# Chunk-batches 7 to 23 of a fused linear-attention and MLP kernel: transposes moved from TensorE to the DMA queue, and a planner that paces the input loads

## The chip, the cores and the metric

The kernel runs on one core of a Trainium2 chip. The metric is device time in microseconds (us) of that core for the whole kernel; the time of a kernel is the median of several executions. One further execution was taken with the hardware profiler, and all durations of single instructions come from it.

## What is computed

A gated linear attention (four batches, eight heads, 768 steps, head size 48) feeds a two-layer MLP with a squared ReLU. Cut to what matters:

```python
def _attn_ref(r, k, v, w, u):                       # all [4, 8, 768, 48], u [8, 48]
    state = zeros((B, H, D, D))
    for t in range(S):
        cur = einsum('bhd,bhe->bhde', u * kt, vt)
        y[:, :, t] = einsum('bhd,bhde->bhe', rt, state + cur)
        state = wt[..., None] * state + einsum('bhd,bhe->bhde', kt, vt)
def _moe_ref(x, w_in, w_out, s, b):                 # x [3072, 384], w_in [384, 2048]
    r = maximum(x @ w_in, 0.0)
    return (s * (r * r) + b) @ w_out
```

`x` is `y` with the heads side by side, one row for each token. Inputs and outputs are float32; the kernel computes in bfloat16 with float32 accumulation.

## The kernel before

**Tiling.** The sequence is cut into 6 chunks of 128 steps. A chunk of one batch is a *chunk-batch*; there are 24 of them, numbered n = 0 to 23, with the batch running fastest, so that chunk-batch n needs the state that n - 4 left. Two chunk-batches make one MLP tile T (256 tokens, 12 tiles).

**One chunk-batch.** SyncE (SP) loads w, r, k and v, 192 KB each (`load`, L225). ScalarE (ACT) takes the logarithm of w (`ln`, L232), TensorE (PE) forms running sums of it (`cum`, L281 to L289), ACT exponentiates them (`expo`, L303), and VectorE (DVE) multiplies them into r and k (`mult`, L313): the result `prd` has time on the partitions. The score product needs it with features on the partitions, so it is transposed into `RK`. There are two ways to do that, chosen by the constant `DTK`:

- n < `DTK`: `trans` (L340) is eight TensorE transposes into PSUM, and `tevac` (L355) is an ACT copy of the 128x1024 result into SBUF;
- n >= `DTK`: `dtrans` (L362) is one DMA crossbar transpose, SBUF to SBUF, issued by SP.

Then come the scores (`mt`, L382, PE), the causal mask (`mask`, L394, DVE), the output (`ymm`, L410 and L419, PE) and its evacuation into `x_sb` (`yevac`, L449, DVE). `x_sb` is transposed into `xT`, the input of the MLP, again in two ways chosen by `DTX`: `xtr` and `xevac` (L497, three TensorE transposes, and L512, an ACT copy), or `dxtr` (L372, one DMA transpose from SP). In the kernel before both constants are 16. GpSimd (POOL) forms the diagonal term from r, k, u and v (L237, L248, L268) and scales the state (L486); it also casts v to bfloat16 (`castv`, which calls `cast`, L636), the engine being chosen by `VBE`.

**The MLP.** For each tile, `g1` is 8 groups of 6 matmuls into `h_ps` (L546), each group followed by `relu` (L559, ACT) and `square` (L571 on DVE or L569 on ACT); `g2` is 8 groups of 4 matmuls into `o_ps` (L584), and after each 128 tokens `oevac` (L594, DVE) and `store` (L608, SP). The weights are loaded by SP after the inputs of chunk-batch 3 and cast once.

**Order.** Nothing is scheduled at run time. Every engine executes its instructions in the order in which they were issued by the program, and that order is the work of a list scheduler, `Plan`. Each operation is registered with `add`: engine, occupancy `occ`, dependences `deps`, buffers that it takes (`takes`), a priority, a latency, and `slack`, which is added to the end of what it depends on. `order` repeatedly takes the operation that can start earliest and writes it out. A DMA has a cost `dma` on one shared modelled DMA queue, whose end time is the variable `dma`. SP is one of the engines: its loads, transposes and stores stand in one fixed order, and a transpose or a store at its head whose input isn't there holds up everything behind it.

Of the kernel before, what the change touches and what calls it, by code (L numbers as in the profile page):

```python
# [18 lines left out]
U_AT = 3.5  # L19
CIE = 'APAP'  # L20
COE = 'DDDD'
VBE = 'P'
WARM = 28.0
DTK = 16
DTX = 16
SQE = 'DA'
SQT = 2
MSL = 0.1
SLACK = 0.3


class Plan:
# [7 lines left out]
        self.ops = {}  # L40

    def add(self, name, eng, occ, fn, args=(), deps=(), takes=(), prio=0.0,
            lat=0.12, port=False, dma=0.0, slack=0.0):
        self.ops[name] = dict(
            name=name, eng=eng, occ=occ, fn=fn, args=args, deps=list(deps),
            takes=list(takes), prio=prio, lat=lat, port=port, dma=dma,
            slack=slack, after=None, n=len(self.ops),
        )

    def order(self):  # L50
        ops = self.ops
        end = {}
        free = {}
        port = 0.0
        dma = 0.0
        held = {tag: [] for tag in self.rings}
        queues = {}
        for o in sorted(ops.values(), key=lambda o: (o["prio"], o["n"])):
            queues.setdefault(o["eng"], []).append(o)
        out = []  # L60

        def ready(o):
            t = 0.0
            for d in o["deps"]:
                if d not in end:
                    return None
                if d == o["after"]:
                    continue
                own = ops[d]["eng"] == o["eng"] and not ops[d]["dma"]
                t = max(t, end[d] - ops[d]["lat"] if own else end[d] + o["slack"])  # L70
            for tag, _ in o["takes"]:
                h = held[tag]
                if len(h) >= self.rings[tag]:
                    for d in h[-self.rings[tag]]:
                        if d not in end:
                            return None
                        t = max(t, end[d] + o["slack"])
            return t

        while any(queues.values()):  # L80
            best = None
            for eng, q in queues.items():
                e = free.get(eng, 0.0)
                pick = None
                for o in q:
                    r = ready(o)
                    if r is None:
                        continue
                    ask = max(r, e)
                    t = max(ask, port) if o["port"] else ask  # L90
                    if pick is None or t < pick[0] - 1e-9:
                        pick = (t, ask, o)
                if pick and (best is None or pick[:2] < best[:2]):
                    best = pick
            assert best is not None, [q[0]["name"] for q in queues.values() if q]
            t, _, o = best
            queues[o["eng"]].remove(o)
            free[o["eng"]] = t + o["occ"]
            if o["port"]:
                port = t + o["occ"]  # L100
            fin = t + o["occ"] + o["lat"]
            if o["dma"]:
                dma = max(dma, t + o["occ"] + 1.0) + o["dma"]
                fin = dma + 0.9
            end[o["name"]] = fin
            for tag, last in o["takes"]:
                held[tag].append(last)
            out.append((t, o))
        self.end = end
        self.last = out  # L110
        return out
# [3 lines left out]
def kernel(  # L115
# [137 lines left out]
    def castv(n):  # L253
        c = cb[n]
        vb = work.tile([128, H, D], BF16, name="vb", tag="vb", bufs=6)
        cast(VBE[n % len(VBE)], vb, c["v"])
        c["vb"] = vb
# [374 lines left out]
    def cast(letter, out, in_):  # L632
        if letter == "A":
            nc.scalar.copy(out=out, in_=in_)  # L634
        elif letter == "P":
            nc.gpsimd.tensor_copy(out=out, in_=in_)  # L636
        else:
            nc.vector.tensor_copy(out=out, in_=in_)
# [18 lines left out]
    for n in range(N):  # L657
# [3 lines left out]
        P = 10.0 * n  # L661
        SL = SLACK if n > 5 else 0.0
        add(("ln", n), "ACT", 0.45, ln, (n,), [("load", n, 0)] + ([("ln", n - 1)] if n else []),
            [("lw", [("cum", n)])], P)
        add(("rkp", n), "POOL", 1.0, pool1, (n,), [("load", n, 1), ("load", n, 2)],
            [("rkp", [("rku", n)])], P, port=True)
        add(("rku", n), "POOL", 1.0, pool1b, (n,), [("rkp", n), "load_u"],
            [("rku", [("cd", n)])], P, port=True)
        e = CAST[VBE[n % len(VBE)]][0]
        add(("vb", n), e, 0.48, castv, (n,), [("load", n, 3)],  # L670
            [("vb", [("ymm", n)] + ([("dmm", n)] if keep else []))], P,
            port=e == "POOL")
# [10 lines left out]
            + ([("mul", n - 1)] if n else []),  # L683
            [("prd", [("tr" if n < DTK else "tev", n)] + ([("dmm", n)] if keep else []))], P - 1, port=True)
        if n < DTK:
            add(("tr", n), "PE", 0.44, trans, (n,), [("mul", n)],
                [("B", [("tev", n)]), ("RK", [("mt", n), ("ymm", n)])], P - 3,
                lat=0.2, slack=SL)
            add(("tev", n), "ACT", 0.92, tevac, (n,), [("tr", n)], [], P - 3)
        else:  # L690
# [8 lines left out]
            + ([("sup", n)] if keep else [("supn", n)]),  # L699
            [("B", [("yev", n)]), ("x", [("xtr" if n < DTX else "xev", n)])], P - 6, lat=0.2, slack=SL)  # L700
        add(("yev", n), "DVE", 0.48, yevac, (n,), [("ymm", n), ("yd", n)], [], P - 7)
        xt = [("xT", [("g1", T, NQ - 1)])] if j == 0 else []
        xd = [("xev", n - 1)] if j else []
        if n < DTX:
            add(("xtr", n), "PE", 0.17, xtr, (n,), [("yev", n)],
# [21 lines left out]
    for T in range(NT):  # L727
        P = BIG + 10 * T
        for i in range(NQ):
# [5 lines left out]
                + ([("gT", [("g2", T, 4 * CPT - 1)])] if i == 0 else []),  # L735
                P, lat=0.2, slack=MSL if T > 1 else 0.0)
            add(("relu", T, i), "ACT", 0.52, relu, (T, i), [("g1", T, i)],
# [4 lines left out]
        for i in range(4 * CPT):  # L742
# [8 lines left out]
            if part == 0:  # L751
                need.append("colsum")
                take = [("h" if T == NT - 1 else "o", [("oev", T, tt)])]
            add(("g2", T, i), "PE", 0.65, g2, (T, i), need, take, P + 1000 + i, lat=0.2, slack=MSL if T > 1 else 0.0)
            if part == 3:
# [10 lines left out]
    for n in range(N):  # L766
        for x in range(4):
            take = {0: [("w", [("ln", n)])],
                    1: [("rk", [("rkp", n), ("mul", n)])], 2: [],
                    3: [("v", [("vb", n), ("yd", n)])]}[x]  # L770
            chain.append((10.0 * n + x, ("load", n, x)))
            add(("load", n, x), "SP", 0.6, load, (n, x), [], take,
                10.0 * n + x, dma=1.03)
    for i in range(NPIECE):
        chain.append((WIN_AT[i] + 0.01 * i, ("li", i)))
        chain.append((WOUT_AT[i] + 0.01 * i, ("lo", i)))
# [81 lines left out]
```

The softmax here doesn't subtract the row's maximum and nothing guards it: scores larger than these inputs give would overflow.

## Time and profile before

| | |
|---|---|
| median of three runs | 200.1 us (200.05 to 200.14) |
| the profiled execution's own time | 200.52 us |
| its span, first to last instruction | 198.7 us |
| granted TensorE clock | 1.000 |
| busy: PE, ACT, DVE, POOL | 187.0, 133.2, 133.1, 114.4 us |
| `trans`, L340: 128 TensorE transposes; `tevac`, L355: 16 copies | 9.8 us; 16.1 us |
| `xtr`, L497: 48 TensorE transposes; `xevac`, L512: 16 copies | 5.3 us; 7.5 us |
| `castv` on POOL, L636: 24 casts | 13.4 us |
| DMA transposes from SP: `RK` 8, `xT` 8 | 3.4 us and 2.3 us from issue to landing (median) |

PE is TensorE's matmuls, PEld its weight loads; SPq is SyncE's queue, where DMAs are issued. A group's line gives busy time, and after it the mean duration of one instruction in nanoseconds. The DMA share is the mean busy share of the core's 16 DMA engines. It is the sum of the packets' own times, and since packets overlap it goes above 1.

### The profile page before, as it was taken

The numbers are of one execution on the slowest core, as the hardware profiler recorded it, in microseconds if no ns is written. First come the engines' busy times: TensorE is split into PE (matmuls) and PEld (weight loads), VectorE is DVE, ScalarE is ACT, GpSimd is POOL, SyncE is SP. The second block draws the span as 40 slices with busy tenths as digits, with TensorE's granted clock in tenths as the row PEclk, the third lists the DMA queues.
The fourth block names the chain that finished last, engine by engine and source line by source line (L and its number), as shares of the span: only waits on it lengthen the run. The fifth ranks groups of instructions, "written<-read, shape, count | busy, mean of one in ns | idle before, by whom it ended". The sixth has DMA issues, their size and how long they took to land.

```text
span 198.7 us, 4921 instructions
## 1 busy us (share of the span) xinstructions
PE 187.0 (94%) x1928; PEld 138.9 (70%) x1928; DVE 133.1 (67%) x212; ACT 133.2 (67%) x240; POOL 114.4 (58%) x144
## 2 busy tenths in 40 slices
PE   6997888979999999999999999999999999999992
PEld 4766567745668777777776786776687778777651
DVE  6476838836977978869787686799787692222221
ACT  3446487745658999999996997690069868768000
POOL 3787932029998899959987788959981000000000
PEclk9999999999999999999999999999999999999999
DMA  6999999979999999999999899999433931111122
GB/s 125 200 175 179 299 394 371 278 145 200 188 156 197 160 195 173 200 234 195 220 169 194 186 202 190 210 236 173 128 82 75 122 98 27 43 40 40 43 79 79
DMA packets 119239, 33.29 MB, mean 168 GB/s; under 512 B 112432, under 2 KB 117680, under 8 KB 119216
## 3 DMA queue, kind: packets, MB, share of 16 engines
q1 hardware_dynamic: 119216, 32.98, 83.0%
q8 instruction: 15, 0.25, 0.6%
q14 instruction: 8, 0.07, 0.1%
HBM read 25.36 MB, written 4.72 MB: 151 GB/s over the span
## 4 chain that ended last, share of the span: by engine, by line
PE 66%; DMA 14%; SPq 11%; ACT 3%; POOL 2%; issue 2%; DVE 1%; POOLq 0%
PE o_ps L584 26%; PE h_ps L546 23%; SPq L225 9%; DMA wi_st<-in_moe_w_in_dram 5%; DMA wt<-in_w_dram 5%; DMA rkt<-in_k_dram 4%; PE mt_ps L382 3%; PE o_psh L584 3%; PE trps L340 2%; PE y_ps L419 2%; PE y_ps L410 2%; PE cums L281 1%; PE cums L284 1%; PE d_ps L435 1%; ACT rh L559 1%
## 5 line engine op out<-in xcount | busy, mean ns | idle before, releaser
L546 PE MATMUL h_ps<-xT,w_in 128*128 128x256 bf16 x576 | 73.9, 273 | 2.0 <-ACT w_in L634 1.4
L559 ACT ACTIVATE rh<-h_ps 128x512 bf16<-128x512 f32 x96 | 56.2, 598 | 23.2 <-PE h_ps L546 21.8
L584 PE MATMUL o_ps<-w_out,gT 128*128 128x384 bf16 x352 | 66.3, 326 | 0.0
L546 PEld LDWEIGHTS <-w_in 128*128 128x128 bf16 x576 | 53.7, 98 | 12.5 <-issue 1.8
L584 PEld LDWEIGHTS <-gT 128*128 128x128 bf16 x384 | 35.8, 98 | 19.2
L571 DVE TENSOR_TENSOR gT<-rh 128x512 bf16<-128x512 bf16 x56 | 29.4, 537 | 14.5 <-ACT rh L559 14.4
L237 POOL TENSOR_TENSOR rkp<-rkt 128x384 f32<-128x384 f32 x24 | 25.1, 1047 | 17.2 <-DMA rkt<-in_k_dram 17.1
L394 DVE TENSOR_TENSOR mt_sb<-mt_ps,tri_strict 128x1024 bf16<-128x1024 f32 x24 | 29.2, 1216 | 1.3 <-PE mt_ps L382 1.3
L268 POOL TENSOR_TENSOR yd<-vt,cd 128x384 bf16<-128x384 f32 x24 | 25.2, 1048 | 4.8 <-DVE cd L262 4.6
L313 DVE TENSOR_TENSOR prd<-rkt,E 128x768 bf16<-128x768 f32 x24 | 24.1, 1004 | 5.6 <-ACT E L303 4.1
L569 ACT ACTIVATE gT<-rh 128x512 bf16<-128x512 bf16 x40 | 25.2, 630 | 1.3
L248 POOL TENSOR_TENSOR rku<-rkp,u_bc 128x384 f32<-128x384 f32 x24 | 24.6, 1025 | 0.4
L303 ACT ACTIVATE E<-cums 128x768 bf16<-128x768 f32 x24 | 19.4, 806 | 7.5 <-PE cums L289 7.4
L594 DVE SCALAR_TENSOR_TENSOR o_sb<-o_ps,s_bc,bconst 128x384 f32<-128x384 f32 x22 | 13.5, 615 | 14.8 <-PE o_ps L584 13.4
L486 POOL TENSOR_TENSOR st<-stmp,l 128x384 bf16<-128x384 bf16 x16 | 18.6, 1164 | 8.3 <-DVE stmp L477 7.9
L355 ACT COPY RK<-trps 128x1024 bf16<-128x1024 bf16 x16 | 16.1, 1008 | 5.5 <-PE trps L340 5.5
L449 DVE TENSOR_TENSOR x_sb<-y_ps,yd 128x384 bf16<-128x384 f32 x24 | 13.3, 552 | 6.7 <-PE y_ps L419 5.2
L262 DVE TENSOR_REDUCE cd<-rku 128x8 f32<-128x384 f32 x24 | 13.0, 542 | 6.8 <-POOL rku L248 6.8
L232 ACT ACTIVATE logw<-wt 128x384 bf16<-128x384 f32 x24 | 12.4, 523 | 7.0 <-DMA wt<-in_w_dram 6.8
L816 PE MATMUL warm_ps<-warm_sb 128*128 128x256 bf16 x104 | 15.1, 294 | 1.1 <-DVE warm_sb L795 1.1
L636 POOL CAST vb<-vt 128x384 bf16<-128x384 f32 x24 | 13.4, 558 | 0.0
L816 PEld LDWEIGHTS <-warm_sb 128*128 128x128 bf16 x104 | 10.2, 105 | 2.7 <-DVE warm_sb L795 1.1
(52 smaller groups left out, 168.5 us busy)
## 6 DMA issues: line engine op xcount, KB each, us to landing
wt<-in_w_dram SPq DMA_DIRECT2D x24, 192.0 KB, 4.5
rkt<-in_r_dram SPq DMA_DIRECT2D x24, 192.0 KB, 4.4
rkt<-in_k_dram SPq DMA_DIRECT2D x24, 192.0 KB, 4.6
vt<-in_v_dram SPq DMA_DIRECT2D x24, 192.0 KB, 4.4
out_dram<-o_sb SPq DMA_DIRECT2D x24, 192.0 KB, 2.2
wi_st<-in_moe_w_in_dram SPq DMA_DIRECT2D x4, 768.0 KB, 8.3
wo_st<-in_moe_w_out_dram SPq DMA_DIRECT2D x4, 768.0 KB, 7.6
u_bc<-in_u_dram SPq DMA_DIRECT2D x1, 192.0 KB, 4.3
```

Of the source, the lines that this page charges most:

```text
L237: nc.gpsimd.tensor_tensor(out=rkp, in0=c["rk"][:, 0].rearrange("t h d -> t (h d)"), in1=c["rk"][:, 1].rearrange("t h d -> t (h d)"), op=AL ...
L248: nc.gpsimd.tensor_tensor(out=rku.rearrange("t h d -> t (h d)"), in0=c["rkp"], in1=u_bc, op=ALU.mult)
L268: nc.gpsimd.tensor_tensor(out=yd, in0=c["v"], in1=c["cd"].unsqueeze(2).to_broadcast([128, H, D]), op=ALU.mult,)
L303: nc.scalar.activation(out=E, in_=ps[:, :, 0:HD], func=AF.Exp)
L313: nc.vector.tensor_tensor(out=prd[:, :, :, 0:D].rearrange("t x h d -> t (x h) d"), in0=c["rk"].rearrange("t x h d -> t (x h) d"), in1=c["E ...
L394: nc.vector.tensor_tensor(out=m.rearrange("s g p t -> s (g p) t"), in0=c["mt_ps"].rearrange("s g p t -> s (g p) t"), in1=tri_strict.unsque ...
L546: nc.tensor.matmul(ps[:, f, :], lhsT=w_in_sb[ft // FPP][:, kt, (ft % FPP) * 128 : (ft % FPP + 1) * 128], rhs=xT[T][:, kt, :], start=(f == ...
L559: nc.scalar.activation(out=rh, in_=hs[T, i], func=AF.Relu)
L569: nc.scalar.activation(out=g, in_=rh, func=AF.Square)
L571: nc.vector.tensor_tensor(out=g, in0=rh, in1=rh, op=ALU.mult)
L584: nc.tensor.matmul(ps, lhsT=gT[T][:, ft, tt * 128 : (tt + 1) * 128], rhs=w_out_sb[ft // FPP][:, ft % FPP, :], start=(ft == 0), stop=(ft == ...
L816: nc.tensor.matmul(warm_ps, lhsT=warm_sb[:, 0:128], rhs=warm_sb, start=True, stop=True)
```

## The change

Five things change. `DTK` goes from 16 to 7 and `DTX` from 16 to 8, so that nine more chunk-batches (7 to 15) have r and k transposed by DMA, and eight more (8 to 15) have x transposed by DMA. `VBE` goes from 'P' to 'AP': the cast of v is done by ACT for even n and by POOL for odd n. `MSL`, the slack that the planner adds before a group of MLP matmuls (tiles 2 and later), goes from 0.1 to 0.2. And the planner gets a new field, `pace`: a load of chunk-batch 4 or later isn't planned before the modelled DMA queue is within 2.0 us of being drained. `pace` adds no instruction and no wait to the program; it acts only through the order in which the operations are written out.

```diff
-VBE = 'P'
+VBE = 'AP'
 WARM = 28.0
-DTK = 16
-DTX = 16
+DTK = 7
+DTX = 8
 SQE = 'DA'
 SQT = 2
-MSL = 0.1
+MSL = 0.2
+PACE = 2.0
 SLACK = 0.3
...
     def add(self, name, eng, occ, fn, args=(), deps=(), takes=(), prio=0.0,
-            lat=0.12, port=False, dma=0.0, slack=0.0):
+            lat=0.12, port=False, dma=0.0, slack=0.0, pace=0.0):
...
-            slack=slack, after=None, n=len(self.ops),
+            slack=slack, pace=pace, after=None, n=len(self.ops),
...
                     ask = max(r, e)
+                    if o["dma"] and o["pace"]:
+                        ask = max(ask, dma - o["pace"])
                     t = max(ask, port) if o["port"] else ask
...
             add(("load", n, x), "SP", 0.6, load, (n, x), [], take,
-                10.0 * n + x, dma=1.03)
+                10.0 * n + x, dma=1.03, pace=PACE if n > 3 else 0.0)
```

## The prediction

> **What bounds the kernel now.** I read the busy shares and slices of the page first, then the groups of instructions, the table of stretches, and last the SyncE queue in order of time.
>
> ```profile
> PE 187.0 (94%) x1928; PEld 138.9 (70%) x1928; DVE 133.1 (67%) x212; ACT 133.2 (67%) x240; POOL 114.4 (58%) x144
> ...
> PE   6997888979999999999999999999999999999992
> ...
> DMA  6999999979999999999999899999433931111122
> ```
>
> PE is full from slice 10 (about 46 us) to 195 us, while the DMA engines are full until about 140 us and nearly empty afterwards. The first 46 us belong to loads and weights; the change hardly touches them.
>
> ```profile
> 60.00:70.00 10.00, 10.00 (x128) 8.16 (x126) 8.18 (x13) 9.69 (x19) 8.51 (x12) 1.00 1.15 179
> ...
> 80.00:90.00 10.00, 10.00 (x122) 7.72 (x119) 7.75 (x12) 9.72 (x20) 7.87 (x11) 1.00 1.08 215
> 90.00:100.00 10.00, 9.68 (x113) 7.50 (x112) 8.32 (x13) 9.42 (x20) 9.47 (x12) 1.00 1.13 206
> 100.00:110.00 10.00, 9.35 (x112) 7.23 (x111) 8.07 (x13) 8.21 (x17) 8.26 (x11) 1.00 1.16 191
> ```
>
> The columns are the stretch, its length, then PE, PEld, DVE, ACT, POOL, clock, DMA share and GB/s. From 60 to 120 us four resources are close to full at once: PE at 93 to 100%, ACT at 82 to 99%, POOL at 79 to 95%, DMA above 1. PE loses about 1 us in 90 to 110. "Busy" could flatter PE, since matmuls overlap; but in the chain of waits the steps follow one another at their full-rate length (6 matmuls of 256 columns 0.66 us, 4 of 384 columns 0.65 us), so PE is bound by throughput. PE's last matmul ends at 195.1 us; DVE and a store finish the span.
>
> ```profile
> L340 PE MATMUL trps<-identity,prd 128*128 128x128 bf16 x128 | 9.8, 219 | 1.1 <-DVE stmp L477 0.6 <-DVE prd L313 0.4
> ...
> L355 ACT COPY RK<-trps 128x1024 bf16<-128x1024 bf16 x16 | 16.1, 1008 | 5.5 <-PE trps L340 5.5
> ...
> L512 ACT COPY xT<-xt_ps 128x384 bf16<-128x384 bf16 x16 | 7.5, 470 | 1.8 <-PE xt_ps L497 1.8
> ...
> RK<-prd SPq DMA_TRANSPOSE x8, 3.4
> xT<-x_sb SPq DMA_TRANSPOSE x8, 2.3
> ```
>
> These are the operations exchanged. The last two are the DMA issues, with median us to landing: the kernel before already runs both transposes for n >= 16.
>
> ```profile
> 126.70 1.33 SPq L225 DMA_DIRECT2D vt<-in_v_dram  x1
> 128.20 1.45 SPq L362 DMA_TRANSPOSE RK<-prd  x1
> ```
>
> This is SyncE's queue (start, duration). 126.7 is the last input load, 128.2 the first transpose. The product that it transposes started on DVE at 113.1 and took 0.95: it waited 14 us behind the loads of later chunk-batches. That order is the plan's.
>
> **What the Trainium skill says.** "VectorE: DVE Perf Modes", section "The three transpose paths", gives a 128x128 bf16 transpose 390 ns on TensorE and 1309 ns by the DMA crossbar. The trace agrees in direction only: eight blocks take TensorE 0.45 us in a stream, and a DMA transpose of the same eight lands in 3.4 us. "Advanced Engine Details and Errata", section "DMA Advanced Topics", says that transposes are as fast as regular DMAs. The trace agrees: below, 256 KB in 1.4 us (about 185 GB/s), where a 192 KB load takes 1.08 us (about 180 GB/s). "DMA: Bandwidth & Descriptors", section "Anatomy of one DMA — SWDGE (gpsimd) path", says that a semaphore wait happens on the issuing sequencer before dispatch: a transpose that waits for DVE stops SyncE, not the DMA engines. In the waits of SyncE's queue, the 8 RK transposes waited 8.1 us and the 8 xT transposes 13.6 us.
>
> **The change part by part.**
>
> *PE.* It loses 9 x 8 transposes for RK and 8 x 3 for x. The price is the time until the next matmul, not the 219 ns of one. In the timeline a group of eight starts at 66.57 and the next matmul at 67.02: 0.45 us. A group of three starts at 69.77, the next matmul at 69.94: 0.17 us. Sum 9 x 0.45 + 8 x 0.17 = 5.4 us, all from an engine that was full.
>
> *ACT.* It loses 9 x 1.008 + 8 x 0.470 = 12.8 us and gains 12 casts of v. The page has no ACT cast of that shape; the logarithm of the same shape and types takes 0.523 us, a quarter of the 128x1536 cast 0.37. I take 0.52: 6.2 us. ACT was at 97% from 60 to 90 us, so 6.6 us less removes a second bound; I count no gain for it beyond the 1 us that PE loses there.
>
> *POOL.* It loses 12 x 0.558 = 6.7 us. Nothing waits long for POOL in the middle; I count nothing.
>
> *DMA engines.* In 152.5 to 155.5 us the share is 0.66 x 3.0 = 1.98 us, for one RK transpose and one store; in 171 to 174 a store alone is 0.18 x 3.0 = 0.54. RK therefore costs 1.44 us of all 16 engines. In 150.5 to 152.4 one xT costs 0.25 x 1.9 = 0.48. The change adds 9 x 1.44 + 8 x 0.48 = 16.8 us to a resource that is full until 130. A load costs 1.08: from the load of w for n = 8 (53.39) to that for n = 15 (85.39), 32.0 us less three stores at 0.54 is 30.4 us for 28 loads.
>
> *SyncE.* It issues 17 more transposes: 9 x 1.28 + 8 x 1.18 = 21 us. A load costs 0.4 us when the queue takes it at once and 0.98 when the queue pushes back, so most of the 21 us replaces push-back. What is queued behind a transpose that waits: every later load and store; who waits for those: ACT's logarithm and POOL's first product.
>
> *Pace.* It changes order only: an RK transpose now stands a few loads behind its product, not sixteen us behind. The modelled queue still never runs dry (a load planned 2.0 us before the drain, with 0.6 issue and 1.0 latency, arrives 0.4 early), so I count no cost in the plan itself.
>
> *MSL.* 0.1 us more slack in the plan only: nothing.
>
> **Does the longer DMA work stay hidden?** At 59 us chunk-batch 8 is loaded or queued. Until the last RK transpose is served the queue must carry 60 loads (64.8 us), 17 RK (24.5), 15 xT (7.2) and about 14 stores (7.6): 104 us, so it is through at 163, and that transpose was issued at about 160. Before, it was issued at 156.3 and the last xT landed at 168.1 (issue 165.8 + 2.3), 11.8 us later. Now the last xT lands at 171.8. The last MLP tile then needs 8 x 0.66 + 5.2 us of matmuls and some 1.5 us of ReLU and square between: 12 us. If PE is to end at 195.1 - 5.4 = 189.7, that xT may land as late as 177.7. So the DMA queue may stand idle for 5.9 us without cost, and for 11.3 us before the gain is gone. The 16 transposes before waited 21.7 us, 1.36 us each, though SyncE had nothing else to do there. A loaded queue covers about 1.1 us of each (median landing of a load 4.4, least 3.3), which leaves 0.26 x 32 = 8 us if all wait so, less where SyncE arrives late. I take 5 to 6 us, just within the cover, and add 1.5 us for PE standing in its fixed order behind an RK or xT that is late, somewhat more than the 1 us that it loses now.
>
> **Sum.** 200.52 - 5.4 + 1.5 = 196.6 against the profiled execution. The median of the runs stands 0.4 lower, so 196.2 us. The cost added is bounded by 0 (all hidden, 194.7, or 193.7 if the present loss in 90 to 110 goes too) and by the slow rival. About 0.2%, or 0.4 us, is what a measurement of this kernel can tell from no change.
>
> **The rivals.**
>
> *The DMA queue becomes the bound (slower).* SyncE stops at a transpose whose product or x isn't ready, the queue behind it drains, and loads come late. Place: SyncE between 60 and 165 us. Price: the idle time for each of the 32 transposes. For it: DMA has no free time before 130, and the load of k for n = 7, issued at 51.19, landed some 3 us before its product began at 58.89. Against it: the load of w for n = 15 was issued at 85.4 while its product began at 109.5, so a large lead built up that can be spent. With 0.5 us idle each, 16 us, the last xT lands at 187.8, PE ends at 199.8, and the time is 204.8. It decides from 11.3 / 32 = 0.35 us each.
>
> *More gain.* PE has no new wait, and ACT's relief and the earlier RK of n = 16 to 20 close the present gaps: 193.7. For it: ACT's 97%. Against it: each transpose is longer than what it replaces.
>
> *The pace does not do what it says.* The model gives a load 1.03, RK 1.0 and a store 0.6 us; the trace 1.08, 1.44 and 0.54. If SyncE drifts behind the plan, transposes still stand behind late loads, and PE waits in order. A drift of 9% on 104 us is 9 us; 5.9 are covered, and 3 remain: 197.7 with the 1.5 above replaced, up to about 199.5 with both.
>
> **How the numbers follow.** Forecast (195 to 198) 0.52; more gain (below 195) 0.09; small gain by drift (198 to 199.7) 0.07; within 0.4 us of no change 0.05; slower by the DMA queue (200.5 to 206) 0.27. So faster 0.68, same 0.05, slower 0.27. The range 194.0 to 203.0 leaves out about 0.04 below and 0.13 above; the likeliest case alone is 195 to 198.
>
> **What would show it.** Right: PE still full from 46 us to its last matmul near 191; ACT near 80% in 60 to 90; RK landing about 5 us after issue and issued within 3 us of its product; DMA full until about 165; the last xT at 172 to 178. Wrong: PE at 9 or below in several stretches between 60 and 165 with `mt_ps` or `h_ps` waiting for a DMA; DMA share well below 1 in 60 to 130; ACT's logarithm waiting for `wt` again and again; the last xT after 183.

## The result and the profile after

The changed kernel takes 208.5 us (207.01 to 209.36, four runs) against 200.12 us (200.05 to 200.61) for the kernel before: a ratio of 1.0405, 95% interval 1.0343 to 1.0467. It is slower by 4%, where 196.2 us and a range up to 203.0 had been predicted. The profiled execution took 207.01 us, with a span of 204.8 us. It was the fastest of the four and had a granted TensorE clock of 1.000, where the other three had 0.983 to 0.992, so the profile shows 6.5 of the 8.4 us by which the median rose. Lines stand three lower in the new file from `order` on (L546 is now L549, and so on).

First the busy shares and the slices of the page, in the form shown of before:

```profile
PE 182.2 (89%) x1827; PEld 132.7 (65%) x1827; DVE 135.0 (66%) x212; ACT 129.6 (63%) x235; POOL 109.8 (54%) x132
...
PE   7977879979999997988999859799997599999992
...
DMA  6979999999999999999999999999889943111122
```

PE lost work, as intended: 187.0 became 182.2 us. But it isn't full any more. Holes run from slice 16 to slice 32, which is about 77 to 164 us (the stretches below show the first and the last at 70 to 80 and 160 to 170), and the DMA engines stay full until about 165 us instead of 140. The groups of instructions and the DMA issues show the exchange itself, and that both transposes now take longer to land (3.4 and 2.3 us before):

```profile
L343 PE MATMUL trps<-identity,prd 128*128 128x128 bf16 x56 | 4.3, 219 | 1.4 <-DVE prd L316 1.4
...
RK<-prd SPq DMA_TRANSPOSE x17, 3.8
xT<-x_sb SPq DMA_TRANSPOSE x16, 3.0
```

Next the table of stretches (length; PE, PEld, DVE, ACT, POOL; clock, DMA share, GB/s):

```profile
60.00:70.00 10.00, 10.00 (x118) 7.63 (x117) 8.47 (x14) 9.57 (x20) 8.89 (x12) 1.00 1.05 183
70.00:80.00 10.00, 8.73 (x95) 6.73 (x95) 8.48 (x12) 7.70 (x15) 8.38 (x11) 1.00 1.22 178
80.00:90.00 10.00, 10.00 (x112) 6.99 (x109) 7.57 (x12) 3.92 (x8) 7.37 (x9) 1.00 1.08 207
90.00:100.00 10.00, 8.76 (x96) 6.37 (x94) 7.85 (x12) 8.50 (x18) 5.87 (x9) 1.00 0.96 197
...
120.00:130.00 10.00, 7.95 (x95) 5.83 (x93) 6.36 (x10) 5.55 (x10) 6.06 (x8) 1.00 0.99 185
...
160.00:170.00 10.00, 7.78 (x85) 5.83 (x84) 7.15 (x11) 7.49 (x13) 4.32 (x5) 1.00 0.71 156
```

Over all eleven stretches from 60 to 170 us PE is busy 98.6 of 110 us. It stands for 11.4 us, where the kernel before stood for 1.0. Less 5.4 us of work and 10.4 us more of standing make 5.0 of the 6 us by which PE's last matmul moved (195.1 to 201.1). ACT fell from 97% in 60 to 90 us to 71%, so it is no bound any more. What ended the idle times is in the waits (total, times, longest), first a line of before, then those of after:

```profile
POOL rkp L237 <- DMA rkt<-in_k_dram: 17.1, 4, 11.6
```

```profile
POOL rkp L240 <- DMA rkt<-in_k_dram: 41.4, 19, 10.2
...
PE mt_ps L385 <- DMA RK<-prd: 6.2, 4, 2.2
...
PE h_ps L549 <- DMA xT<-x_sb: 2.6, 4, 1.2
```

PE waits for the two things that now come by DMA, and POOL waits for input loads 41.4 us instead of 17.1: what comes through SyncE's queue is late. The last xT was issued at 176.8 and landed at 179.1, eleven us later than before. One place shows what such a wait costs, PE's own order (start, duration, and in brackets the idle time before):

```profile
159.43 0.81 PE L587 MATMUL o_ps<-w_out,gT 128*128 128x384 bf16 x4
162.47 0.40 PE L385 MATMUL mt_ps<-RK 48*128 48x128 bf16 x8 [2.22 <-DMA RK<-prd]
162.80 1.48 PE L549 MATMUL h_ps<-xT,w_in 128*128 128x256 bf16 x12
164.12 0.81 PE L587 MATMUL o_ps<-w_out,gT 128*128 128x384 bf16 x4
```

PE stood 2.22 us for one RK. The `o_ps` group at 164.12 belongs to tile 7, whose `h_ps` matmuls were over at 142.6 us (counting 48 for each tile) and whose last square ended at 144.0: work that was ready stood behind work that wasn't. From the last xT to PE's end are 22.0 us, in which PE is full with MLP work left over.

SyncE's queue in order of time (start, duration):

```profile
92.65 0.57 SPq L228 DMA_DIRECT2D wt<-in_w_dram  x1
93.27 0.57 SPq L228 DMA_DIRECT2D rkt<-in_r_dram  x1
93.95 1.95 SPq L365 DMA_TRANSPOSE RK<-prd  x1
96.00 0.52 SPq L611 DMA_DIRECT2D out_dram<-o_sb  x1
96.58 0.42 SPq L228 DMA_DIRECT2D rkt<-in_k_dram  x1
97.10 1.32 SPq L375 DMA_TRANSPOSE xT<-x_sb  x1
```

There are hardly any gaps: from 60 to 160 us the longest is 0.51 us. Summed over that stretch SyncE's DMA issues take 90.8 us, and the 0.09 us or so between any two make up most of the rest. 14 RK take 1.95 us each there, 12 xT 1.38, 59 loads 0.66 (0.93 before). The product for the RK issued at 93.95 was ready 2.5 us earlier:

```profile
90.47 0.96 DVE L316 TENSOR_TENSOR prd<-rkt,E 128x768 bf16<-128x768 f32 x1 [1.25 <-ACT E L306]
```

The same holds for every RK issued between 74 and 164 us: its product had been finished for 1.6 to 4.1 us. The products wait for SyncE, not SyncE for the products.

### The profile page after: what moved, and what is told of

Its sections match the earlier page's. It is cut to its first block, busy times and chain, and to the rows that moved or that the text cites. A ratio compares the mean times of both kernels' runs of the same rounds, so it can differ in the third digit from the quotient of the medians.

```text
span 204.8 us, 4735 instructions
## 1 busy us (share of the span) xinstructions
PE 182.2 (89%) x1827; PEld 132.7 (65%) x1827; DVE 135.0 (66%) x212; ACT 129.6 (63%) x235; POOL 109.8 (54%) x132
## 4 chain that ended last, share of the span: by engine, by line
PE 49%; DMA 26%; SPq 12%; DVE 5%; POOL 3%; issue 2%; ACT 1%; DVEq 0%; POOLq 0%
PE o_ps L587 19%; PE h_ps L549 18%; DMA RK<-prd 8%; SPq L228 8%; DMA rkt<-in_k_dram 7%; DMA wi_st<-in_moe_w_in_dram 6%; DMA xT<-x_sb 3%; PE o_psh L587 3%; PE mt_ps L385 2%; DMA vt<-in_v_dram 2%; SPq L365 2%; POOL rkp L240 1%; DVE gT L574 1%; PE y_ps L422 1%; PE cs_ps L616 1%
## 5 line engine op out<-in xcount | busy, mean ns | idle before, releaser
L549 PE MATMUL h_ps<-xT,w_in 128*128 128x256 bf16 x576 | 72.9, 272 | 4.5 <-DMA xT<-x_sb 2.6
L549 PEld LDWEIGHTS <-w_in 128*128 128x128 bf16 x576 | 53.7, 97 | 16.0 <-issue 4.2
L240 POOL TENSOR_TENSOR rkp<-rkt 128x384 f32<-128x384 f32 x24 | 28.1, 1172 | 41.4 <-DMA rkt<-in_k_dram 41.4
L574 DVE TENSOR_TENSOR gT<-rh 128x512 bf16<-128x512 bf16 x56 | 30.0, 552 | 10.3 <-ACT rh L562 10.1
L316 DVE TENSOR_TENSOR prd<-rkt,E 128x768 bf16<-128x768 f32 x24 | 25.5, 1064 | 7.9 <-ACT E L306 4.3
L597 DVE SCALAR_TENSOR_TENSOR o_sb<-o_ps,s_bc,bconst 128x384 f32<-128x384 f32 x22 | 13.5, 613 | 10.9 <-PE o_ps L587 10.8
L235 ACT ACTIVATE logw<-wt 128x384 bf16<-128x384 f32 x24 | 12.5, 521 | 11.3 <-DMA wt<-in_w_dram 11.0
L489 POOL TENSOR_TENSOR st<-stmp,l 128x384 bf16<-128x384 bf16 x16 | 15.2, 952 | 3.5 <-DVE stmp L480 3.5
L819 PE MATMUL warm_ps<-warm_sb 128*128 128x256 bf16 x99 | 14.6, 292 | 1.1 <-DVE warm_sb L798 1.1
L385 PE MATMUL mt_ps<-RK 48*128 48x128 bf16 x192 | 9.5, 219 | 6.6 <-DMA RK<-prd 6.2
L637 ACT CAST vb<-vt 128x384 bf16<-128x384 f32 x12 | 6.1, 511 | 13.3 <-DMA vt<-in_v_dram 13.3
L385 PEld LDWEIGHTS <-RK 48*128 48x128 bf16 x192 | 5.5, 94 | 12.4 <-DMA RK<-prd 8.0
```

What stands on the lines that cost most here:

```text
L240: nc.gpsimd.tensor_tensor(out=rkp, in0=c["rk"][:, 0].rearrange("t h d -> t (h d)"), in1=c["rk"][:, 1].rearrange("t h d -> t (h d)"), op=AL ...
L316: nc.vector.tensor_tensor(out=prd[:, :, :, 0:D].rearrange("t x h d -> t (x h) d"), in0=c["rk"].rearrange("t x h d -> t (x h) d"), in1=c["E ...
L385: nc.tensor.matmul(ps[:, sg, p, :], lhsT=c["KT"][pr, p, :], rhs=c["RT"][pr, p, :], start=(p == 0), stop=(p == HP - 1),)
L549: nc.tensor.matmul(ps[:, f, :], lhsT=w_in_sb[ft // FPP][:, kt, (ft % FPP) * 128 : (ft % FPP + 1) * 128], rhs=xT[T][:, kt, :], start=(f == ...
L574: nc.vector.tensor_tensor(out=g, in0=rh, in1=rh, op=ALU.mult)
```

## The experiments

Three theories at the start: **A**, the DMA queue is full and the added transposes are what fills it; **B**, the queue could carry them, but PE's fixed order was written by a planner that prices DMAs too low, so that PE stands behind inputs that come later than planned; **C**, the new order as such (pace, casts, slack) costs the time. A fourth, **H**, came from the prediction: SyncE stops for late products and the queue runs dry. A fifth, **S**, came from the profile after: SyncE's issuing is full. All ratios are to the kernel before, run beside each version on the same chip. The expectations call `DTK` the first constant and `DTX` the second.

**1. Everything but the added transposes.**

```diff
-DTK = 7
-DTX = 8
+DTK = 16
+DTX = 16
```

> The changed kernel with both constants back at 16: pace, the ACT casts and the larger MLP slack stay, the 17 added DMA transposes go. Theory A (the DMA queue is the bound from 60 to 165 us, because of the added 16.8 us of transposes): the loss goes, 198.5 to 201 us, PE idle after 60 us at most 3 us. Rival C (the new order written by pace and slack costs the time, whoever transposes): 204 us or more.

Measured: 199.99 us, ratio 0.9985 (0.9966 to 1.0004). C falls. Pace, the ACT casts and the larger slack together change nothing that is measured, and PE stands only 0.9 us from 60 to 160 us. The loss comes with the added transposes and the order that is written around them. Whether the pace helps or harms once the transposes are added was not tried.

**2. True DMA prices in the plan.**

```diff
-            add(("tev", n), "SP", 1.2, dtrans, ...  dma=1.0
+            add(("tev", n), "SP", 1.3, dtrans, ...  dma=1.44
-            add(("xev", n), "SP", 0.7, dxtr, ...  dma=0.4
+            add(("xev", n), "SP", 1.2, dxtr, ...  dma=0.48
-                10.0 * n + x, dma=1.03, pace=...
+                10.0 * n + x, dma=1.08, pace=...
```

> The changed kernel, but the planner prices DMAs as the trace does: load 1.08 instead of 1.03, RK transpose 1.44 and 1.3 of SyncE instead of 1.0 and 1.2, xT 0.48 and 1.2 of SyncE instead of 0.4 and 0.7. Same work, other order. Theory A (queue full): at most 2 us better, 205 to 208. Rival B (the queue could carry it, but PE's fixed order was written for an earlier arrival of the inputs, so PE stands behind score products while MLP work is ready): at least 5 us better, 197 to 202.

Measured: 203.05 us, ratio 1.0137 (1.0082 to 1.0191). That lies between the two expectations, nearer to B: the same transfers in another order take 5.4 us less. The profiled execution took 201.83 us, 5.2 us less than that of the changed kernel at the same granted clock of 1.000. Its last xT was issued at 181.1 and landed at 183.4, later than in the changed kernel, and yet PE ends earlier, at 196.1: the tail is 12.7 us instead of 22.0. PE's order at that place:

```profile
181.73 2.60 PE L587 MATMUL o_ps<-w_out,gT 128*128 128x384 bf16 x15
184.17 2.97 PE L549 MATMUL h_ps<-xT,w_in 128*128 128x256 bf16 x24
```

It starts on the last tile as soon as its x is there, with no older tile in between; the MLP work was done while the inputs were awaited. So one part of the loss is order. Whose order is not separated: SyncE's queue is written anew as well as PE's, and an RK is now issued 0.8 us after its product ends, on average, instead of 2.1. Nor was the order changed in some other way with the prices left wrong, so that a new order helps is shown, and that it helps because its prices are true rests on this pair and that of experiment 5. Against the kernel before, the attention itself is still late.

**3. Cheap loads.** Eight runs of 192 bytes for each partition become one run of 1536 bytes; the kernel then reads other elements of its inputs.

```diff
+        if n >= 8:
+            view = src[bb].rearrange("h s d -> (h s d)").rearrange(
+                "(t h d) -> t h d", h=H, d=D)[t0 : t0 + L]
```

> The changed kernel, with the w, r, k and v loads of chunk-batches 8 to 23 taken as contiguous rows of 1536 bytes instead of eight runs of 192 bytes: as many bytes, same order, but other elements of the inputs, so the output is not the reference's. A load should then cost the queue about the 0.54 us of a store instead of 1.08, 64 x 0.5 = 32 us less in all. Theory A: the PE waits of 11 us between 70 and 170 us vanish, 194.5 to 197.5 us, below the kernel before. Rival C (order): 203 us or more. A third view, that the latency of a single transpose (3 to 4 us) is what PE waits for: 201 to 206.

> Control for the one before: the kernel before, with the same contiguous loads for chunk-batches 8 to 23 (other elements of the inputs are read). Its PE is full from 46 us on, so theory A expects little: 198.5 to 200.2 us. If it gains 3 us or more, the loads limited the kernel before too, and the comparison with the changed kernel must be made against this one.

Measured: the changed kernel with cheap loads 194.38 us, ratio 0.9724 (0.9664 to 0.9783); the kernel before with them 198.8 us, 0.9946 (0.9919 to 0.9972). A foresaw both, the first to 0.1 us of its range. The stretch from 60 to 160 us, first of the changed kernel, then of the changed kernel with cheap loads:

```profile
60.00:160.00 100.00, 90.81 (x962) 67.13 (x959) 75.90 (x113) 70.24 (x136) 69.64 (x81) 1.00 1.06 188
```

```profile
60.00:160.00 100.00, 99.03 (x1071) 74.66 (x1070) 83.22 (x126) 79.98 (x151) 73.61 (x85) 1.00 0.89 204
```

PE is full again and the DMA share falls below 1, although the order is the one written with the low prices. Two things follow. The saving on PE is real: with the loads out of the way the change gains 198.8 - 194.4 = 4.4 us over its control. And this order does harm only where transfers are late. A transpose still takes 3.3 us to land (median of the xT), and it doesn't matter here. Loads of 1536-byte runs also cost SyncE less to issue (0.49 us each instead of 0.66), so this run alone doesn't say whether the engines or SyncE were the limit; run 7 looks at that.

**4. Only one kind of transpose moved.** `DTK` 7 and `DTX` 16; then `DTK` 16 and `DTX` 8.

> The changed kernel with the x transposes back on TensorE for n = 8 to 15 (second constant 16): only the nine RK transposes are added to the DMA queue, 13.0 of the 16.8 us. Theory A+B (loss in proportion to the DMA time that the plan underprices): the 8.3 us of loss shrink to about 6, 204 to 207 us. If the loss is per transpose, by SyncE's stops (9 of 17 left): 203 to 205. If the small x transposes alone did the harm: about 200.

> The changed kernel with the RK transposes back on TensorE for n = 7 to 15 (first constant 16): only eight x transposes are added, 3.8 us of DMA time. In proportion to DMA time: 200 to 202 us. By number of SyncE stops (8 of 17): 203 to 205.

Measured: RK only 203.17 us, 1.0118 (1.0072 to 1.0163); x only 206.36 us, 1.0249 (1.0184 to 1.0313). The first agrees with a loss for each transpose, but the second missed both of its expectations by far: 3.8 us of DMA time cost more than 13.0 us. The loss is not in proportion to DMA time, nor to the number of transposes. In the x-only profile the last xT was issued at 167.5 and landed at 169.8, only 1.6 us later than before, so its attention isn't late at its end; still PE ends at 200.6 and stands 7.1 us between 60 and 160. A version that loses its time in the middle, and not at the end, points to order, and the next run tests that.

**5. Only x moved, with true DMA prices.**

```diff
-DTK = 7
+DTK = 16
```
and the prices of experiment 2.

> Only the x transposes moved (first constant 16, second 8), with the true DMA prices in the plan. With the old prices this version took 206.4 us although its last xT landed at 170 us, two us later than in the kernel before. Rival B (PE's fixed order, written for DMAs that are too cheap, is the loss): 199 to 201.5 us. If the small x transposes hold up the queue by themselves: 205 to 207.

Measured: 201.22 us, 1.0018 (0.9994 to 1.0041). That is what B foresaw: the same 16 x transposes, in another order, cost 0.2% instead of 2.5%. The last xT lands at 173.8 us, 4.0 us later than with the old prices, and PE still ends 5.9 us earlier, at 194.7, so the loss of this version is its order. PE in the stretch from 60 to 160 us, first with the old prices, then with the true ones:

```profile
60.00:160.00 100.00, 92.90 (x1038) 71.32 (x1036) 79.76 (x117) 79.53 (x150) 73.54 (x86) 1.00 1.05 178
```

```profile
60.00:160.00 100.00, 98.38 (x1103) 74.49 (x1102) 83.31 (x123) 82.27 (x154) 72.91 (x86) 1.00 1.01 179
```

The DMA engines moved as much in both (178 and 179 GB/s); PE stood 7.1 us in one and 1.6 in the other. Which of the corrected prices matters was not tried.

**6. No late inputs for the transposes.** Each DMA transpose reads what the chunk-batch before its own has left.

```diff
-            out=RK, in_=c["prd"]...
+            out=RK, in_=cb[n - 1]["prd"]...
-            out=xT[T][:, :, j * L : (j + 1) * L], in_=cb[n]["x"]
+            out=xT[T][:, :, j * L : (j + 1) * L], in_=cb[n - 1]["x"]
```

> The changed kernel, but every DMA transpose reads the product, or the x, of the chunk-batch before its own, which is ready earlier: same transfers, same order, no stop of SyncE for a late input (the output is not the reference's, since RK and xT hold the neighbour's data). Rival H (SyncE's stops let the queue run dry, 7 us): 200 to 204. Theory A (the queue's capacity): 206.5 to 208.5, within 2 us of the changed kernel.

Measured: 208.67 us, 1.0392 (1.0362 to 1.0422), no change against 1.0405. H falls. That agrees with the queue shown above: the products are ready before SyncE comes to them, and there are no gaps to win back. An RK still takes 1.73 us to issue instead of 1.95, so little of that time is waiting for an input.

**7. Less issuing on SyncE.** The order of the changed kernel stays, but ACT issues the v loads of n = 8 to 23.

```diff
-        nc.sync.dma_start(
+        (nc.scalar if which == 3 and n >= 8 else nc.sync).dma_start(
```

> The changed kernel, in the same written order, but the 16 loads of v for n = 8 to 23 are issued by ACT instead of SyncE: the same DMA work, about 10 us less issuing on SyncE, about 9 us more on ACT. Theory S (SyncE's issuing is what is full: it issues 17 to 19 us of every 20, and its loads no longer meet push-back, 0.57 us instead of 0.95): 202 to 205 us. Theory A (the 16 DMA engines are full): 207 to 209 us, or more if ACT is held up.

Measured: 206.51 us, 1.0267 (1.022 to 1.0314): a gain, between the two expectations and short of what S expected. The stretch from 60 to 160 us:

```profile
60.00:160.00 100.00, 90.49 (x961) 66.94 (x959) 77.40 (x115) 72.71 (x139) 68.46 (x81) 1.00 1.26 195
```

With two queues to feed them the DMA share rises from 1.06 to 1.26, but what they move only from 188 to 195 GB/s. And although 14 loads have left SyncE there, its issues still take 87.8 us of the 100, because each of the rest became longer (an RK 2.00 us). So SyncE's issuing was a limit, and right behind it are the engines; how much of a long issue is SyncE's own time and how much is waiting for a full queue was not separated. Cheap loads take about as much issuing off SyncE as this run does (59 loads x 0.17 us = 10 us) and gain 14 us; this run gains 2. Most of the gain of cheap loads is therefore the engines' time, not SyncE's: with the order as it was written, A holds for the largest part.

**8. Order and issuing together.** True prices, and v from ACT.

> The full change with true DMA prices in the plan, and the v loads of n = 8 to 23 issued by ACT. If order and SyncE's issuing are the two losses: 196 to 199 us, below both kernels. If the DMA engines are full: 202 to 204, as with the true prices alone.

Measured: 200.79 us, 1.0004 (0.9982 to 1.0026), between the two expectations. It removes the whole loss but gains nothing. The last xT still lands at 181.6 us. SyncE's issues take 70 of the 100 us from 60 to 160, with gaps up to 2.2 us: in this version it does stop for transposes whose input isn't there. Whether its remaining lateness is those stops or the engines was not separated.

**9. Fewer transposes, with both remedies.** As 8, with `DTK` 11.

> A version meant to beat both: true DMA prices in the plan, v loads of n = 8 to 23 issued by ACT, and RK by DMA from n = 11 instead of 7 (x from 8): 5 RK and 8 x transposes added, 11.0 us of DMA time instead of 16.8, and 3.6 us of PE work removed instead of 5.4. If the queue has room for about 10 us once order and issuing fit: 197 to 199 us. If DMA work added before the last load costs as much as it saves on PE, as in the full change: 200 to 201.5.

Measured: 199.64 us, 0.9947 (0.9924 to 0.9969), against 200.6 us for the kernel before. It beats the kernel before by half a per cent; against experiment 1, which adds no transposes at all (0.9966 to 1.0004), it isn't clear of noise. An earlier attempt, both constants at 12 with true prices and all loads on SyncE, did not:

> A version meant to beat both: true DMA prices in the plan as in the run before, both constants at 12, so that eight DMA transposes (4 RK, 4 x, 7.7 us of DMA time) are added instead of 17. If the queue has 5 us and more to spare once the order fits: 197 to 199.5 us, faster than before. If any added DMA work before the last load costs: 200 to 203.

Measured: 201.53 us, 1.0051 (1.0023 to 1.0079), as expected if any added DMA work costs.

## Why the prediction was wrong

**Right: the work that moves.** ACT's copies shrank by 12.7 us (12.8 priced), the cast of v takes 0.511 us on ACT (0.52 taken), PE's busy time fell by 4.8 us (5.4 priced), and cheap loads let 4.4 us of PE's saving appear.

**Nearly right: how late the attention ends.** The account of the queue gave a last xT at 171.8 us if the queue never idles, and 5 to 6 us of idling were allowed. It landed at 179.1, 7.3 us later. That is beyond the 5.9 us said to be covered, but by 1.4 us only, and short of the 11.3 us from which the gain was to be lost. That it came so near is in part luck: the 5 to 6 us were to be SyncE standing for late inputs, and experiment 6 shows that it doesn't stand.

**Wrong, and the step that failed: "that xT may land as late as 177.7".** It counted the tail after the last xT as the 12 us of one tile, as if PE would use up all older MLP work before. The changed kernel has 22.0 us there, and the kernel before had 27 us already (168.1 to 195.1), as its profile shows. The step looked at the end of the attention alone; but inputs are late all the way from 70 us on, and PE, which executes in a written order, paid each delay where it occurred, even with ready work behind it. The term of the sum, "1.5 us for PE standing in its fixed order", is 10.4 us (11.4 in all, less the 1.0 of before). The run with true prices has a tail of 12.7 us with a later xT: the 12 us are right for the order that was written there, and not for that of the changed kernel.

**Wrong: what SyncE's 21 us cost.** They were said to replace push-back mostly. The loads did become cheaper to issue, by 59 x 0.27 = 16 us from 60 to 160 us, but an RK costs 1.95 us to issue among loads instead of the 1.28 taken from a nearly empty queue, and the queue ended without a gap. Moving 16 loads away brought 1.4% of the kernel back. The price of a transpose was also judged against a slow thing: 256 KB in 1.44 us are as fast as a load in runs of 192 bytes (192 KB in 1.08), but half as fast as a store in runs of 1536 bytes (192 KB in 0.54), all three by the prediction's own estimates.

**The rivals.** The slow one had the place and the sign right: the DMA queue becomes the bound, 204.8 us. Its mechanism, 0.5 us of stop for each transpose, is shown wrong. The 21.7 us of SyncE waits that priced it were misread: most of those "waits" end inside the issue of the transpose itself, so they are issuing and not standing (SyncE had gaps of 7.0 us in all before these transposes), and in the loaded queue of the changed kernel hardly any standing is left. The rival in which the order doesn't fit, with 198 to 199.5 us, had the mechanism of one large part at about half its size (3 us, where true prices gave back 5.4): it charged drift only beyond the cover of 5.9 us, and there was no such cover. Its sum was also short: with the xT counted, the plan's prices make 93.2 us of what the trace makes 104.1, a drift of 10.9 us instead of 9. Of the signs of being wrong, PE at 9 or below with `mt_ps` and `h_ps` waiting for a DMA, and ACT's logarithm waiting for `wt` (11.0 us), came true; a DMA share well below 1 before 130 us and a last xT after 183 did not.

In sizes, against the kernel before: order about 2.7% (1.0405 to 1.0137 with true prices), relief of SyncE about 1.4% (to 1.0267 alone, 1.3% more on top of true prices). With both remedies the ratio is 1.0004, and what uses up the 2.7% that PE gives back was not separated: the attention stays late, and PE stands 3.9 us after 60 us, where it stood 1.0 before. With cheap loads the ratio is 0.9724.

## What to carry to other kernels

Taking work off the fullest engine can cost more than it saves when what takes its place comes later than the written order assumes: here PE, with 5.4 us less to do, stood 10.4 us longer, and new prices for three kinds of DMA, taken from the trace, gave back 5.4 us with the same transfers. So the prices of a plan are worth checking against the trace, in a loaded queue and not in an idle one. A resource that is already full for two thirds of the kernel, such as this DMA queue, should be asked first how much room it has, both in its engines and in the sequencer that feeds it. And slack at the end of a chain was no cover here for delays in its middle, because the order was fixed.

## What the runs showed of the hardware that was not expected

Issuing a DMA transpose is long: with an idle queue 1.18 us on SyncE for an xT and 1.23 to 1.3 us for an RK, and 1.95 us on average for the RK (256 KB) among loads, where a 192 KB load takes 0.66 us. A sequencer that issues such a mixture can be as full as the DMA engines behind it: SyncE's issues took 90.8 of 100 us. The same 192 KB in runs of 1536 bytes instead of 192 bytes made the changed kernel 14 us faster at equal bytes and took SyncE 0.49 us instead of 0.66 to issue. And a DMA share of 1.26 moved only 4% more bytes a second than one of 1.06, while a share of 0.89 with long runs moved more than either (204 GB/s): the share is no measure of bytes moved.

A long wait of PE may cost more than itself. In the profiles of experiments 6 and 7 PE stood 2.99 and 2.42 us for one RK near 160 us, and just after it four matmuls of 384 columns took 1.48 and 1.49 us instead of 0.81:

```profile
162.60 0.40 PE L385 MATMUL mt_ps<-RK 48*128 48x128 bf16 x8 [2.99 <-DMA RK<-prd]
162.94 2.15 PE L549 MATMUL h_ps<-xT,w_in 128*128 128x256 bf16 x12
164.88 1.48 PE L587 MATMUL o_ps<-w_out,gT 128*128 128x384 bf16 x4
```

The granted clock was 0.80 from 165 to 170 us in experiment 6, and 0.66 from 160 to 165 in experiment 7. In the changed kernel's profile the wait of 2.22 us at the same place was followed by 0.81 us and a clock of 1.00. Whether the wait is what lowers the clock was not tested, but the three executions of the changed kernel that were not profiled had the lower clocks and took 1.5 to 2.4 us longer.
